# Quarters of two weight matrices on a second transfer queue, a longer run of zero products at the start, key features in half pieces, and another hand-written order

## The chip, the core and the metric

The kernel runs on one core of one Trainium2 chip. Its engines work side by side and meet only at semaphores: PE multiplies matrices, DVE and ACT do elementwise work, POOL (GpSimd) does a little of the same, SP issues transfers, and 16 DMA engines move the data. The metric is the device time of one execution in microseconds, as a median over runs.

## The reference, cut to what matters

Everything is float32 except the sketches S1, S2 and the four weight matrices, which arrive as float64 and are turned into float32 on the chip.

```python
# attention: q, k, v are (4, 4, 1088, 32); S1, S2 are (8, 32)
phi(x) = outer product of (S1 x) and (S2 x), 64 numbers for each token
kv  = sum over tokens of phi(k) v       # 64 x 32 for each head
z   = sum over tokens of phi(k)         # 64 for each head
x   = (phi(q) kv) / (phi(q) z + 1e-6)   # (4352 tokens, 128)
# feed-forward: w1, w2 are 128 x 1024, w3 is 1024 x 1024, w_out is 1024 x 128
out = (((x w1) * (x w2)) w3) w_out
```

The kernel first multiplies w3 by w_out (a 1024 x 128 matrix, here "the folded weight"), so that the feed-forward part is three products for each slice of 128 hidden columns: a, b, and the sum over slices o.

## The kernel before, in words

**The work as steps.** `make_steps` registers about 970 small steps, each with a name and a few instructions. The kernel then runs through the string `ORDER` and emits the steps in that order (lines 1173 to 1181); a scheduling dependency ties each instruction to the one before it on the same engine, so `ORDER` is the program order of PE, ACT, DVE, POOL and SP at once. There is no planner at run time: an engine that reaches an instruction whose data is not there waits, and everything behind it on that engine waits too.

**Names.** `kB.` steps make the keys' sums of batch B (0 to 3): `max`, `g`, `lead`, `rest` split the keys into a leading part and a rest (L471 to L484, DVE); `gram` multiplies keys with keys on PE (L497, L498: 36 calls each way, every float32 product being two matrix instructions and two weight loads); `Gm` to `Gb`, `T`, `N` turn that into scaling matrices in small DVE and PE steps; `kT`, `ab`, `abc` or `abt` make the sketches, `kp` the features (L515, on POOL for batch 0 and on DVE for the others), `kv` and `kvr` the sums with v on PE. `kr0` and `kr1` are the last 64 tokens of batches 0,1 and 2,3. `qG.` steps make the attention output of token group G (0 to 7, two to a batch, and `r` for the remainders); their last step `qG.xT` (ACT) writes the transposed activations that the feed-forward products of group G read. `gG.Ca`, `gG.Cb` are the products a and b of slice C (L1099, L1109), `gG.Cc` copies a out of PSUM (ACT), `gG.Cm` multiplies (DVE, L1115), `gG.Co` adds to the output (L1121). `s.` steps prepare the sketches; `s.split` runs on POOL.

**Weights.** Slice n of the weights is loaded into one of three buffers called `raw` as raw 64-bit words by `wN.load`: n = 0, 1 are halves of w1 and w2, n = 2 is w_out, n = 3 to 10 are 128 rows of w3. The last two kinds are loaded by four transfers of 32 partitions each (L303, L310), all issued by SP. ACT reads the words in `wN.c` (L325), `wN.s` (L329), `wN.m` (L333), DVE joins them in `wN.j` (L344) and `wN.a` (L349). For w3, `fN.t` transposes on DVE (L377) and `fN.m` makes the folded weight on PE (L383). A `raw` buffer can be loaded again when its `c` and `m` are done. Keys and values have one buffer each (`k`, `v`), so `k1.load` must wait until `k0.gram1` and the other readers of batch 0 are done.

**The start.** Before the first feed-forward product nothing else can feed PE for long, and `warmN` steps (L176) put bf16 products of zeros between its waits; `WARM` holds how many.

Of the kernel before, what the change touches and what calls it, by code (L numbers as in the profile page):

```python
# [25 lines left out]
WARM = [15, 5, 3, 1, 6, 15, 4, 2, 5]  # L26

BY_PE = ()

# [4 lines left out]
c.zeros v0.zero c.ident c.mask k0.zero k0.load0 k0.loadr k0.load1 s.load c.act q0.load s.zero v0.loadr w0.load  # L34
k0.max0 w1.load k0.max1 k0.nat1 kr0.load warm0 k0.tr1 k0.g0 k0.g1 k0.lead0 k0.kT1 k0.lead1 kh1.load k0.nat0
k0.rest0 s.words k0.rest1 warm1 k0.gram0 s.pair q0.tr s.split k0.gram1 q1.tr s.lead w0.c v0.load q0.max k0.tr0
k0.Gm s.T k0.Gt k0.kT0 w0.j k1.zero s.P k1.load q0.l2 s.blk k0.Ga s.blkh warm2 k0.ab1 k0.Gb q0.l1 s.Pp k1.loadr
q0.A0 k0.ab0 w2.load q0.rm k0.T0 k0.T1 k0.abc0 kr0.tr k0.abc1 k0.Ta k0.kp0 warm3 q0.C0 w1.c k1.kT1 q1.max w1.m
k0.Tb q0.sma q0.restT kr0.kT k0.Ts w0.m k0.kp1 warm4 k0.kv0 k1.max k0.N0 k0.N1 w0.s q0.sta w3.load k0.Na q0.sha
w1.s k0.Nh k0.Nb q0.sla kr1.load warm5 q0.A1 k0.Nl k0.Nf kr0.ab q0.sca k0.kv3 q0.smy kr0.abc q0.al k0.kv1 kr0.kp  # L40
q0.sty q0.C1 q0.phi w4.load q1.l2 k0.kv2 k0.kvr v1.zero q1.l1 q0.shy warm6 q0.pt0 k0.kvm q0.C1t q0.sly k0.kzt
q0.pt1 q0.pc0 q0.scy v1.load q0.p01 q1.A0 k0.kz q0.pc1 q0.p2 warm7 q0.x q1.rm q0.p12 w1.j w3.c q0.dn q0.de w2.c
q1.sm q1.C0 q0.rc q1.st q0.xs w0.a q0.xt q0.xT q1.sh w2.m k1.g w1.a warm8 g0.1a g0.1b w2.j g0.1c w5.load w2.s
k1.lead g0.0a g0.1m kr1.tr g0.6a kr1.kT g0.0c k1.rest w3.s g0.0b w2.a kr1.ab g0.6b g0.6c w3.m g0.5a g0.0m g0.6m
g0.7a g0.5c w6.load q1.sl kr1.abc k1.kT0 g0.5b w3.j g0.7b g0.5m q1.load w4.c k1.gram0 w3.a g0.7c k1.ab w4.m
q1.sca q1.scy f0.t k1.gram1 w5.c w7.load k1.gram2 q1.al q1.p01 g0.2a q1.p2 w4.s k2.zero g0.7m q1.p12 kh2.load
g0.4a w4.j g0.2c q1.dn f0.m g0.4c w4.a w6.c k2.load q1.de k1.Gm f1.t v1.loadr w5.m g0.2b g0.4b q1.rc g0.2m f0.o
w5.s w10.load f1.m k1.Gt q1.bs q2.tr w6.m q1.phi g0.0o k1.abt f1.o w6.s w8.load q1.pt1 k1.Ga q2.max q1.pt0 w5.j
g0.3a q1.pc0 g0.4m q1.pc1 k2.loadr q1.x k1.kp1 g0.1o q1.xT w5.a q2.l2 g1.1a g0.3c k1.Gb g0.3b f2.t g1.1c q2.l1
k1.T0 k1.T1 g1.5a g0.3m f2.m k1.Ta g1.5c k1.kp0 w7.c w7.m w6.j g1.1b k1.Tb g1.6a w6.a f2.o w7.s w9.load k1.kv0  # L50
g1.1m k1.kv2 k1.kv3 k1.kv1 w8.c w7.j k1.kvr g0.2o f3.t w8.s g1.5b w7.a f3.m g1.6c k1.kvm k1.Ts g1.5m w8.j g1.6b
f3.o f4.t k1.N0 w9.c k1.N1 g1.4a g1.6m g1.4b k1.Na g1.4c k2.max w9.s f4.m g1.4m w8.m k1.Nb g1.0a k2.g w9.j f4.o
g1.0b k1.Nf q2.rm g1.0c w10.c k2.lead g0.3o k1.Nl k1.Nh g1.3a g1.0m k2.rest g1.2a g1.3c w9.m g0.4o q3.tr w8.a
k2.gram0 k2.gram1 k2.kT1 q2.C0 f5.t k2.kT0 k2.gram2 q3.max q2.A0 k2.ab k3.zero k3.loadr v2.zero w9.a kr1.kp
q3.l2 v2.load f5.m g1.2c q2.At q3.l1 q2.Ct q2.sm q3.rm g1.7a f5.o w10.s q2.st f6.t g1.3b w10.m g0.5o q2.sh w10.j
f6.m q2.sl g1.3m q2.sca q2.scy q2.al q3.A0 q2.p01 f6.o q3.C0 g1.7c w10.a g1.2b q2.p2 f7.t g1.7b q2.p12 q2.dn
f7.m k2.Gm q2.de q1.restT q2.rc q2.load q2.bs q3.At v2.loadr q3.Ct g0.6o kh3.load q2.phi f7.o g0.7o k2.abt
q2.pt0 k3.load g0.oT q2.pt1 g1.2m k1.kzt g1.0o g0.st k1.kz q2.pc0 q3.sm g1.7m q2.pc1 g1.2o k2.Gt q3.st g1.5o
q3.sh q3.sl q2.x k2.kp0 g1.3o q2.xT q3.sca k3.max g2.7a g2.1a k3.g k2.Ga q3.p01 k2.kp1 g2.7b g2.1c g2.7c g1.1o
q5.tr g1.6o q5.max q3.al k3.lead g1.4o q4.tr g1.7o k2.Gb g2.5a g2.7m q4.max g2.1b q3.scy k3.rest g2.5b k2.kv0  # L60
q3.p2 k3.gram0 g2.1m q3.p12 g2.5c k3.gram1 k3.kT0 g2.5m k2.kv3 k2.kv1 k2.kv2 g1.oT k2.kvr k3.gram2 v3.zero
v3.load k2.kvm q3.dn k2.T0 k2.T1 g2.2a k3.Gm k2.Ta g2.3a k2.Tb v3.loadr g2.2c k2.Ts q3.de q4.l2 g1.st q3.rc
k2.N0 q3.bs k2.N1 q3.phi g2.2b q4.l1 g2.3c g2.0a g2.2m k2.Na g2.3b g2.0c k2.Nb q3.pt1 k2.Nh k3.kT1 g2.0b g2.3m
q3.pt0 q4.rm g2.6a k2.Nf g2.0m g2.4b g2.6c k3.Gt k2.Nl q3.pc0 g2.4a q3.pc1 q3.x q4.A0 q3.xT q4.C0 g2.4c k3.ab
g2.0o k3.abt g2.4m g3.3a g2.6b g2.2o g2.6m k3.Ga g3.3b q4.At g3.3c q4.sm g2.5o q4.st q4.Ct g3.2b g3.3m q4.sh
g3.2a k3.kp0 k2.kzt g2.1o g3.2c q5.l2 g3.2m g3.4a k3.kp1 g2.4o g3.4c k2.kz q4.sl q5.l1 g3.4b q4.sca k3.Gb g3.6a
q4.p01 g3.4m q5.A0 q4.al k3.T0 k3.T1 g3.1a k3.Ta q5.At g2.6o q4.scy g3.1c q5.sm g3.6c q5.rm g3.1b q2.restT
q3.load g2.3o g3.1m k3.Tb g3.0b q4.p2 q4.p12 g3.6b q4.dn q4.de k3.Ts q5.st g3.0a q5.sh q3.restT g2.7o g3.0c
g3.0m q5.C0 q4.rc g3.6m q5.sl k3.kv0 k3.kv1 g2.oT k3.kv3 k3.kv2 q4.bs k3.kvr g2.st q5.Ct g3.5a q5.sca q5.p01
g3.7b g3.5c q6.tr g3.0o q4.phi g3.5b k3.kvm q7.tr g3.3o q5.al qr.max g3.2o q5.scy qr.l2 g3.5m q5.p2 q4.pt0  # L70
q5.p12 g3.6o q5.dn q4.pc0 qr.l1 g3.7a q4.pt1 g3.7c g3.1o q4.pc1 g3.7m q4.x q5.de q5.rc q5.bs g3.4o q4.xT k3.N0
k3.N1 g4.3b k3.Na qr.rm g4.3a k3.Nh k3.Nf k3.Nb q5.phi g4.0a g4.3c g3.5o g4.3m g4.0c q5.pt0 g4.5a g4.5b g4.5c
q5.pc0 q5.pt1 g4.5m g3.7o q5.pc1 g4.0b g4.4a g4.0m g3.oT g4.4b g4.4c g3.st g4.2a g4.4m k3.Nl g4.7a q6.max g4.0o
qr.C0 qr.A0 q5.x qr.Ct qr.At q7.max g4.5o q5.xT qr.sm g4.2c g4.2b g4.7c q6.l2 g4.7b g4.2m q6.l1 qr.st g5.0a
g4.7m qr.sh g4.6a g5.0c qr.sl q6.rm k3.kzt g4.6b qr.sca k3.kz g4.6c qr.al qr.p01 g5.0b g4.6m q6.A0 g5.0m q6.C0
q6.At qr.scy qr.p2 q7.l2 g4.1a qr.p12 qr.dn qr.de qr.rc g4.2o g4.1c q7.l1 g4.6o q7.rm g4.3o q6.sm qr.bs g4.1b
g5.2a g4.1m qr.phi g5.2b g5.2c q6.st qr.pt0 q6.sh g5.7a qr.pc0 q6.sl q6.Ct g4.4o g5.2m qr.pt1 q6.sca g4.1o
qr.pc1 q6.al g5.7c g5.7b q7.A0 q7.C0 q7.At q6.p01 g5.7m qr.x q6.scy q6.p2 q6.p12 g5.5a q6.dn q6.de q6.rc g4.7o
g5.5c q6.bs g5.6a g4.oT g5.6b g4.st g5.6c qr.xT g5.0o g5.6m q7.sm g5.5b q7.st g5.4a g5.5m q7.sh g5.4b g5.4c
q6.phi g5.5o q7.Ct g5.1a g5.4m q6.pt0 g5.3b q6.pc0 q6.pt1 g5.3a q6.pc1 g5.1c q6.x g5.3c g5.3m g5.1b q6.xT g5.6o  # L80
g5.1m q7.sl g5.4o q7.sca g5.1o g5.3o g6.1a g5.2o g6.1c g6.1b g6.4a g6.1m q7.scy g6.6a q7.al g6.4c q7.p01 g6.4b
g6.6c g5.7o g6.4m q7.p2 g6.6b g5.oT q7.p12 g6.0a g5.st g6.6m q7.dn g6.0b g6.0c g6.5a g6.0m g6.3a g6.5c g6.3b
g6.3c g6.5b g6.3m q7.de gr.2b g6.5m g6.0o q7.rc q7.bs g6.2a q7.phi gr.2a g6.2c g6.4o gr.2c gr.2m g6.6o g6.2b
gr.0a g6.2m q7.pt1 gr.0b gr.0c q7.pt0 gr.0m g6.7a q7.pc0 g6.7b g6.7c q7.pc1 q7.x g6.7m g6.5o q7.xT g7.1a g7.1b
g7.1c g7.0a g7.1m g6.2o g7.3a g6.3o g7.3c g7.0c g7.0b g6.1o g7.0m g6.7o g7.3b g6.oT g7.4a g6.st g7.3m g7.4b
g7.4c g7.2b g7.4m g7.2a g7.6a g7.2c g7.2m g7.0o g7.6c g7.2o g7.5a g7.1o g7.5c g7.6b g7.7a g7.6m g7.5b g7.7c
gr.5a g7.5m g7.7b gr.6a g7.7m g7.5o gr.6c gr.5c g7.3o gr.6b gr.5b g7.6o gr.5m gr.6m gr.4b gr.4a g7.4o gr.4c
gr.4m gr.1b gr.1a g7.7o gr.1c gr.1m gr.3a g7.oT gr.3b gr.3c gr.7a g7.st gr.3m gr.0o gr.7c gr.6o gr.2o gr.5o
gr.7b gr.3o gr.7m gr.1o gr.4o gr.7o gr.oc gr.ot gr.oT gr.st
# [7 lines left out]
def make_steps(ctx, tc, q, k, v, S1, S2, moe_w1, moe_w2, moe_w3, moe_w_out, out):  # L97
    nc = tc.nc
    dve, act, pe, pool, sp = nc.vector, nc.scalar, nc.tensor, nc.gpsimd, nc.sync
    B, H, S, D = q.shape  # L100
# [191 lines left out]
    def conv(n):  # L292
# [3 lines left out]
        def _():  # L296
# [4 lines left out]
            elif n == 2:  # L301
                for t in range(4):
                    sp.dma_start(raw[n][t * 32:(t + 1) * 32],  # L303
                                 bass.AP(tensor=moe_w_out.tensor, offset=moe_w_out.offset + t * 256 * DM,
                                         ap=[[DM, 32], [32 * DM, NC], [1, DM]]))
            elif n - 3 in BY_PE:
                sp.dma_start(raw[n], moe_w3[(n - 3) * 128:(n - 2) * 128])
            else:
                for t in range(4):
                    sp.dma_start(raw[n][t * 32:(t + 1) * 32],  # L310
                                 bass.AP(tensor=moe_w3.tensor, offset=moe_w3.offset + (n - 3) * 128 * DF + t * 256,
                                         ap=[[DF, 32], [32 * DF, 4], [1, 256]]))
# [898 lines left out]
```

## Time and profile before

| What | us |
|---|---|
| Median of 13 runs | 281.68 (279.6 to 284.61) |
| The profiled execution | 282.83 |
| Its span, first to last instruction | 281.0 |
| PE busy in the span | 265.0 |
| DVE busy | 186.0 |
| ACT busy | 113.1 |
| POOL busy | 11.4 |
| First feed-forward product starts | 33.59 |
| Last feed-forward product ends | about 275.4 |

A row of a timeline gives the start, the length, the engine, the line, the operation with its output and inputs, the count, and in brackets the idle time before it with what ended that time. In a table of windows, PEclk is the share of full speed that the throttle granted to PE, and the DMA share is how busy the 16 DMA engines were.

### The profile page before, as it was taken

The page shows a single profiled execution, that of the slowest core. Times are in us where ns is not written, and L with a number is a line of the kernel's source. Part 1 is how long each engine was busy: PE and PEld are TensorE (multiplying, and loading weights), DVE is VectorE, ACT ScalarE, POOL GpSimd, SP SyncE. Part 2 cuts the span into 40 slices and gives each one's busy share as a digit, 9 for nine tenths or more (in the row PEclk, how much of TensorE's full clock was granted, in tenths as well). Part 3 has the DMA queues.
Part 4 walks back from the last instruction along what each step waited for, and adds up shares of the span by engine and source line. Part 5 has one row for each costly group of instructions (what it writes and reads, how often), then busy time and mean ns, then how long its engine had stood idle before and what let it go on. Part 6 is the DMA issues. An engine that isn't in the chain of part 4 may idle for free.

```text
span 281.0 us, 5298 instructions
## 1 busy us (share of the span) xinstructions
PE 265.0 (94%) x2134; PEld 149.5 (53%) x2134; DVE 186.0 (66%) x420; ACT 113.1 (40%) x180; POOL 11.4 (4%) x41
## 2 busy tenths in 40 slices
PE   7997998799997999979999999999999999999992
PEld 5885746456657663534444545444544445344571
DVE  4779989498989989956398855476773265121430
ACT  3675698667592422033231143163123222322121
POOL 2451000000001000000000000000000000000000
PEclk9999999799999999979999999999999999999999
DMA  7999999998600273050002200200020020001011
GB/s 211 314 248 217 214 198 249 218 219 168 127 1 9 75 193 79 2 119 0 2 0 80 39 1 0 37 2 1 2 37 0 0 41 0 0 15 22 0 20 38
DMA packets 32168, 22.50 MB, mean 80 GB/s; under 512 B 21392, under 2 KB 26640, under 8 KB 32144
## 3 DMA queue, kind: packets, MB, share of 16 engines
q1 hardware_dynamic: 31600, 21.64, 34.6%
q10 hardware_dynamic: 544, 0.52, 0.6%
q8 instruction: 17, 0.28, 0.5%
q14 instruction: 7, 0.06, 0.1%
HBM read 19.93 MB, written 2.23 MB: 79 GB/s over the span
## 4 chain that ended last, share of the span: by engine, by line
PE 82%; DMA 9%; SPq 3%; issue 3%; ACT 1%; DVE 0%; ACTq 0%
PE a_ps L1099 22%; PE b_ps L1109 21%; PE ps_o L1121 20%; DMA raw<-in_moe_w_dram 6%; PE ps_w3o L383 6%; PE ps_x L1065 3%; DMA raw<-in_moe_w_out_dram 3%; PE ps_c L810 3%; PE ps_ph L1020 2%; PE ps_g L492 2%; PE ps_kv L590 1%; SPq L1077 1%; PE ps_ab L565 1%; DMA out_dram<-oT 1%; SPq L300 1%
## 5 line engine op out<-in xcount | busy, mean ns | idle before, releaser
L1115 DVE TENSOR_TENSOR ab<-ffa,b_ps 128x512 f32<-128x512 f32 (+1 forms) x72 | 46.8, 652 | 62.8 <-PE b_ps L1109 48.6
L1104 ACT COPY ffa<-a_ps 128x512 f32<-128x512 f32 (+1 forms) x72 | 39.9, 564 | 98.7 <-PE a_ps L1099 93.1
L1099 PE MATMUL a_ps<-xT,w 128*128 128x512 f32 (+1 forms) x144 | 70.4, 585 | 0.4 <-ACT xT L1057 0.4
L1109 PE MATMUL b_ps<-xT,w 128*128 128x512 f32 (+1 forms) x144 | 69.7, 578 | 0.0
L1121 PE MATMUL ps_o<-ab,w3o 128*128 128x512 f32 (+1 forms) x144 | 67.4, 574 | 0.0
L1109 PEld LDWEIGHTS b_ps<-xT,w 128*128 128x128 f32 x144 | 26.8, 193 | 28.9 <-issue 25.3
L1099 PEld LDWEIGHTS a_ps<-xT,w 128*128 128x128 f32 x144 | 26.1, 192 | 26.5 <-issue 20.1
L1121 PEld LDWEIGHTS ps_o<-ab,w3o 128*128 128x128 f32 x144 | 26.1, 190 | 26.2 <-issue 23.1
L383 PEld LDWEIGHTS ps_w3o<-wo,w3T 128*128 128x128 f32 x128 | 16.2, 199 | 6.8 <-issue 5.5
L383 PE MATMUL ps_w3o<-wo,w3T 128*128 128x128 f32 x128 | 16.9, 286 | 2.5 <-issue 2.5
L325 ACT ACTIVATE cv_c<-raw 128x1024 f32<-128x1024 f32 x11 | 12.9, 1181 | 6.6 <-DMA raw<-in_moe_w_dram 5.4
L333 ACT ACTIVATE sg<-raw 128x1024 uint16<-128x1024 uint32 x11 | 15.1, 1377 | 0.0
L329 ACT CAST sg<-cv_c 128x1024 f16<-128x1024 f32 x11 | 14.9, 1372 | 0.0
L1026 ACT COPY pT<-ps_ph 128x512 f32<-128x512 f32 (+1 forms) x18 | 9.9, 567 | 7.9 <-PE ps_ph L1020 7.9
L492 PE MATMUL ps_g<-kk 128*32 128x64 f32 x288 | 10.9, 233 | 1.9 <-issue 1.9
L492 PE MATMUL ps_g<-k,kk 128*32 128x32 f32 x288 | 10.4, 200 | 1.5 <-issue 1.5
L1020 PEld LDWEIGHTS ps_ph<-ident,ph 128*128 128x128 f32 x68 | 8.3, 140 | 6.6 <-issue 4.6
L176 PE MATMUL idle_ps<-zeros 128*128 128x256 bf16 x56 | 9.9, 326 | 1.6 <-DVE zeros L151 1.1
L492 PEld LDWEIGHTS ps_g<-kk 128*32 128x32 f32 x288 | 9.0, 114 | 3.6 <-issue 2.4
L492 PEld LDWEIGHTS ps_g<-k,kk 128*32 128x32 f32 x288 | 9.7, 117 | 2.0 <-issue 2.0
L1020 PE MATMUL ps_ph<-ident,ph 128*128 128x128 f32 x68 | 10.0, 273 | 0.0
L377 DVE STREAM_TRANSPOSE w3T<-w3c 128x1024 f32<-128x1024 f32 x8 | 9.9, 1234 | 0.0
(199 smaller groups left out, 291.4 us busy)
## 6 DMA issues: line engine op xcount, KB each, us to landing
raw<-in_moe_w_dram SPq DMA_DIRECT2D x32, 256.0 KB, 7.9
qh<-in_q_dram SPq DMA_DIRECT2D x4, 544.0 KB, 4.0
raw<-in_moe_w_dram SPq DMA_DIRECT2D x4, 512.0 KB, 6.5
out_dram<-oT SPq DMA_DIRECT2D x32, 64.0 KB, 2.0
kh<-in_k_dram SPq DMA_DIRECT2D x12, 128.0 KB, 7.4
k<-in_k_dram SPq DMA_DIRECT2D x3, 512.0 KB, 7.6
v<-in_v_dram SPq DMA_DIRECT2D x12, 128.0 KB, 2.8
raw<-in_moe_w_out_dram SPq DMA_DIRECT2D x4, 256.0 KB, 7.9
```

The source lines that it names most:

```text
L176: pe.matmul(t[:, :256], zeros[:, :128], zeros, start=True, stop=True)
L325: act.mul(shape(x["c"], 1, True), words(1).bitcast(F32), 2.0 ** -112)
L329: act.copy(bview(sign_bits[n % 2].bitcast(F16)[:, 1:], [[2, 1024]]), x["c"])
L333: act.mul(shape(sign_bits[n % 2].bitcast(U16), 2, True), words(0).bitcast(U32), 2.0 ** -29)
L383: pe.matmul(t["o"], w3T[ko][:, c], wo[:, c], start=c == 0, stop=c == NC - 1)
L492: pe.matmul(o[h * D:(h + 1) * D], lhs, rhs, start=start, stop=stop, skip_group_check=True)
L1020: pe.transpose(t[:, j * 128:(j + 1) * 128], ph_cols(j, p), ident)
L1099: pe.matmul(x["a"][:, :w], w_of(0, c), xT[g][:, c0:c0 + w], start=True, stop=True)
L1104: act.copy(x["s"][:, :w], x["a"][:, :w])
L1109: pe.matmul(x["b"][:, :w], w_of(1, c), xT[g][:, c0:c0 + w], start=True, stop=True)
L1115: dve.tensor_mul(ab_sb[g, c][:, c0:c0 + w], x["s"][:, :w], x["b"][:, :w])
L1121: pe.matmul(o_ps[g][:, :n], w3o[:, c], ab_sb.pop((g, c))[:, :n], start=c == 0, stop=c == NC - 1)
```

## The change

1. `wN.load` of w_out and w3 keeps quarters 0 and 2 on SP. A new step `wN.load2` issues quarters 1 and 3 from POOL.
2. `k0.kp0` and `k0.kp1`, one POOL instruction each of 1024 columns, become `kp0a`, `kp0b`, `kp1a`, `kp1b` of 512 columns.
3. `WARM` is changed: 22 zero products at the start instead of 15, and 54 instead of 56 in all.
4. `kT` is kept per batch, so that batch 1's transposed keys can be made while batch 0's are in use.
5. `ORDER` is new throughout. At the start, the key sums' products of batch 1 (`k1.ab`, `k1.gram0` to `gram2`) stand ahead of the first feed-forward product (now `g0.7a`); before, they stood behind twelve of them. `w1` is loaded ahead of `w0`, both after batch 0's values. `k1.load` is ahead of `w0` and `w2` on SP. The folds come in the order f0, f2, f1, f4, f3, f5, f6, f7.

```diff
-WARM = [15, 5, 3, 1, 6, 15, 4, 2, 5]
+WARM = [22, 4, 5, 1, 10, 1, 6, 2, 3]
+QUEUE2 = "pool"
...
-c.zeros v0.zero c.ident c.mask k0.zero k0.load0 k0.loadr k0.load1 s.load c.act q0.load s.zero v0.loadr w0.load
-k0.max0 w1.load k0.max1 k0.nat1 kr0.load warm0 k0.tr1 k0.g0 k0.g1 k0.lead0 k0.kT1 k0.lead1 kh1.load k0.nat0
-k0.rest0 s.words k0.rest1 warm1 k0.gram0 s.pair q0.tr s.split k0.gram1 q1.tr s.lead w0.c v0.load q0.max k0.tr0
-k0.Gm s.T k0.Gt k0.kT0 w0.j k1.zero s.P k1.load q0.l2 s.blk k0.Ga s.blkh warm2 k0.ab1 k0.Gb q0.l1 s.Pp k1.loadr
-q0.A0 k0.ab0 w2.load q0.rm k0.T0 k0.T1 k0.abc0 kr0.tr k0.abc1 k0.Ta k0.kp0 warm3 q0.C0 w1.c k1.kT1 q1.max w1.m
-k0.Tb q0.sma q0.restT kr0.kT k0.Ts w0.m k0.kp1 warm4 k0.kv0 k1.max k0.N0 k0.N1 w0.s q0.sta w3.load k0.Na q0.sha
...
+c.zeros s.zero k0.zero k0.load0 k0.loadr c.ident k0.load1 c.mask s.load c.act q0.load kh1.load k0.max0 s.words
+k0.g0 k0.lead0 k0.nat1 s.pair k0.nat0 warm0 k0.tr1 k0.rest0 s.split q0.tr k0.tr0 k0.kT1 k0.max1 s.lead k0.gram0
+k0.kT0 q0.max q1.tr q0.l2 s.P s.T k0.g1 q0.restT k0.lead1 s.blk k0.rest1 warm1 k0.ab1 s.Pp k0.gram1 k0.abc1
+q0.l1 k0.kp1a k1.kT0 k0.ab0 k0.Gm v0.zero v0.load v0.loadr kr0.load w1.load k0.Gt q0.rm k0.abc0 k0.Ga s.blkh
+w1.m k0.Gb k0.kp0a warm2 q0.A0 k0.T0 k1.kT1 k0.T1 q0.C0 k0.Ta k0.kp1b q1.max k0.Tb kr0.tr q0.sma warm3 k0.N0
+kr0.kT k1.zero k1.loadr k1.load w0.load w2.load q1.load k0.Ts k0.kp0b w1.c k1.max k0.kv0 k0.kv2 k0.N1 kr0.ab
+w3.load w3.load2 k0.Na kr0.abc w1.s q0.sta kr1.load k0.Nh k1.g k0.Nf k0.Nb q0.sha warm4 q0.A1 k0.Nl k0.kv3 w1.j
+kr0.kp q0.C1 q0.smy q1.l2 k0.kv1 q0.sla q0.sty q0.sca w2.load2 warm5 k0.kvr q0.shy q1.l1 q0.C1t q0.al w0.c
+q0.sly q0.phi warm6 k1.ab w0.m q0.p01 warm7 q0.pt1 q0.scy k0.kvm q0.pt0 q0.p2 q1.rm w5.load w5.load2 k0.kzt
+k0.kz q0.p12 q0.pc0 warm8 q1.C0 k1.lead q0.pc1 w3.c q0.dn k1.rest q1.A0 w0.s q0.x q0.de q1.sm w0.j q0.rc w2.c
+k1.gram0 k1.abt q0.xs k1.gram1 q1.st w1.a q0.xt k1.gram2 q0.xT q1.sh w3.s g0.7a w0.a k2.zero k2.loadr g0.7b
...
-                for t in range(4):
-                    sp.dma_start(raw[n][t * 32:(t + 1) * 32],
-                                 bass.AP(tensor=moe_w3.tensor, offset=moe_w3.offset + (n - 3) * 128 * DF + t * 256,
-                                         ap=[[DF, 32], [32 * DF, 4], [1, 256]]))
+                quarter(sp, 0)
+                quarter(sp, 2)
...
+        if n >= 2 and n - 3 not in BY_PE:
+            @step(f"w{n}.load2")
+            def _():
+                for t in (1, 3):
+                    quarter({"pool": pool, "act": act, "sp": sp}[QUEUE2], t)
...
-                @step(f"k{b}.kp{half}")
-                def _(half=half):
-                    f["kp", half] = sb("kp", [128, 4 * H, r, r], bufs=2)
-                    x = f["abs", half]
-                    k_phi(f["kp", half], x[:, 0], x[:, 1], pool)
+                for part in "ab":
+                    @step(f"k{b}.kp{half}{part}")
+                    def _(half=half, part=part):
+                        if part == "a":
+                            f["kp", half] = sb("kp", [128, 4 * H, r, r], bufs=2)
+                        x, g = f["abs", half], slice(0, 2 * H) if part == "a" else slice(2 * H, 4 * H)
+                        k_phi(f["kp", half][:, g], x[:, 0, g], x[:, 1, g], pool)
```

## The prediction

> **What bounds the kernel now.** I read the page first, then the chain of waits in order of time, then the windows at its holes, then the timelines of the start.
>
> ```profile
> span 281.0 us, 5298 instructions
> ## 1 busy us (share of the span) xinstructions
> PE 265.0 (94%) x2134; PEld 149.5 (53%) x2134; DVE 186.0 (66%) x420; ACT 113.1 (40%) x180; POOL 11.4 (4%) x41
> ```
>
> PE sets the end. From the first feed-forward product (33.59) the chain stays on PE to 275.4 and has three holes over 1 us, all called "issue": PE waited for no data.
>
> ```profile
> 47.40 1.00 PE ps_w3o L383 x9
> 48.41 2.55 issue
> 50.95 1.86 PE ps_w3o L383 x7
> ...
> 86.88 1.51 issue
> ...
> 119.73 1.92 issue
> 122.20 3.25 PE a_ps L1099 x4
> ```
>
> The first hole lies inside one step (f0.m, 16 products, cut at nine). Counting products by the program, the holes stand near numbers 602, 988 and 1376, and a smaller one (0.52 us at 26.1) at 349: about 3, 5, 8 and 11 times 128. Each product is a matrix instruction and a weight load, so these are multiples of 256 instructions; the instruction queue moved 17 packets of 16 KB for PE's 4268. I read it so: crossing a multiple starts the fetch of the block after the next multiple, and a hole comes when PE gets there first. Crossing to resumption: 17.0 to 26.6 and 43.3 to 50.95 (9.6 and 7.7 us, DMA engines full), 84.3 to 88.39 and 117.6 to 121.9 (4.1 to 4.3, DMA idle). Each of the last three comes after a gram, 144 products within some 2.7 us. After two holes the clock is slow, too (columns: window, busy PE, PEld, DVE, ACT, POOL, PEclk, DMA share, GB/s):
>
> ```profile
> 50.90:52.60 1.70, 1.65 (x7) 1.65 (x8) 0.00 (x0) 0.05 (x1) 0.00 (x0) 0.51 1.06 217
> 52.60:56.00 3.40, 3.40 (x11) 1.62 (x11) 1.46 (x4) 2.72 (x3) 0.00 (x0) 0.74 1.07 228
> ```
>
> Here 7 fold products took 1.86 us instead of 0.78, four halves of b 2.55 instead of 1.72, the next fold 1.97 instead of 1.78: 2.1 us lost.
>
> The 33.6 us before the first product are a chain of short steps. Its timelines show a gap of 0.88 us behind the zeros, and DVE blocked while POOL makes key features: a 32x32 operation that takes 0.18 elsewhere took 1.74 and ended with POOL's first of two.
>
> ```profile
> 1.06 3.38 PE L176 MATMUL idle_ps<-zeros 128*128 128x256 bf16 x15 [1.06 <-DVE zeros L151]
> 5.33 1.09 PE L529 MATMUL ps_kt<-ident,nat 128*128 128x128 f32 x4 [0.88 <-ACT nat L523]
> ```
>
> ```profile
> 16.27 3.87 POOL L515 TENSOR_TENSOR kp<-kab 128x1024 f32<-128x1024 f32 x2 [4.02 <-ACT kab L546]
> ...
> 16.54 1.74 DVE L137 SCALAR_TENSOR_TENSOR T_p<-T_g,T_t 32x32 f32<-32x32 f32 x1
> ...
> 20.98 1.35 DVE L140 TENSOR_REDUCE k_g<-k 128x1 f32<-128x1152 f32 x1 [0.79 <-DMA k<-in_k_dram]
> ```
>
> **1. The start, -2.0 us.** Fifteen zero products took 3.38 us, so 22 reach to 6.0, when the first transposes are ready (nat1 at 4.57, now behind s.words' 0.75): no gap. Gram products run at 40 ns until 9.9 us and at 22 ns after it; all 144 at 22 ns are 3.2 us instead of 4.4. But gram1 now stands behind s.T and ab1: s.words now precedes the copies on ACT (data in by 4.4, 0.75 long), so s.pair moves from 8.1 to 5.3 on DVE and takes 0.5; s.split takes 3.4 on POOL (8.68 to 12.1 before, 5.8 to 9.2 now); s.P and s.T take 1.0 on PE, so s.T ends at 10.2; s.blk 0.3 and k0.rest1 0.7 on DVE end at 11.2; gram1 takes 1.6 and ends at 13.1 (before 11.84). Then on DVE s.Pp 1.4 and kT0 0.6 to 13.25, the G steps with q0.rm 1.5 to 14.75, kT1 0.6 to 15.4, T's first two operations to 15.8. Its shift is the operation that took 1.74 above: it now waits for half a feature instruction (0.98, half of 1.96) that started at 15.4, not for a whole one, and is done at 16.5 (before 18.28). q1.max 0.6 and Tb 0.35 end at 17.45, k1.max (1.3) when the keys land, some 18.3, so k0.Na starts at 19.6 (before 22.45). From there DVE's own sum decides: Na to the end of xs was 8.65 us; added are k1.lead 0.8, k1.rest 1.27, w0.j 0.6, k1.abt 0.62: 11.95, so xs ends at 31.6 (before 31.1). On PE q1.C0 (1.75) and x (2.2) end at 30.9, gram0 and gram1 (0.6 to 1.05 each) at 32.1 to 33.0, xt 0.45, copy 0.58: first product at 33.7 to 34.6, I take 34.3, 0.7 later. In exchange the 2.7 us that k1.gram and ab hold at 42.72 to 45.42 are gone from the packed part. Net -2.0; bounds -3.5 (gram in 0.6, no wait) and +1.5 (next point and transfers).
>
> **2. The fetch holes, -6.2 and +0.5.** In the new order number 476 (4th multiple) falls in k1.gram1, 604 in f0.m, 14 us later: over 9.6, so the hole of 2.55 and its 2.1 of slow clock go. From 860 to 988 lie f5.m 1.8, four products 3.4, two grams 1.2 to 2.1: at least 6.4, over 4.1, so 1.51 goes. From 1244 to 1372 there are 2 to 3 us (k3's three grams and T), under 4.2: that hole stays with its slow clock, 0. New risk: 348 falls at about 23.2, 476 at about 31.8; with 7.7 to 9.6 the block comes at 30.9 to 32.8, so 0 to 1.0, I take 0.5, more if the clock falls.
>
> **3. DVE as second bound, +1.5.** With PE earlier, folds are due earlier: f5.m about 77 (before 89.68), f6.m 86 (94.14), f7.m 90 (99.16). DVE needs 2.9 us a slice (0.6, 1.13, 1.16). Summing its steps from rows, DVE has 27.6 us done at 34.3, 6.7 idle, and 69 done at the end of f5.t: 75.7 if never idle again, 1.3 ahead of PE; 0.6 ahead at f6. Before, DVE idled 3.7 of the 60 us from 60 to 120. I take 1.5, bounds 0 and 4. k1.lead and k1.rest are covered by PE's own start; that cover is in the sum.
>
> **4. The second queue, 0.** Before, PE waited for no weight, so faster loading alone saves nothing. SP issued a quarter in 0.31 to 1.01 us, landing 4.9 to 10.4 later. Behind w3.load2 on POOL stand kr0.kp (for kvr) and w2.load2; it waits for w1.c (18.7, as w3.load did at 18.79). SP holds w0, w2 and q1 behind k1.load, which waits for gram1 (13.1, before 14.35). A POOL issue is in no row: nearest are SP's 0.3 to 1.0 and POOL's 1.96; two of w3's land by 18.8 + 4 + 7.8 = 30.6 at the dear end. ACT then has w3.c, w0.s, w2.c (3.7 us) ahead of xT, needed at 33.4: bounds 0 and +1. I stay at the SP row.
>
> Whether two queues are faster: loads of 128 partitions moved 341 GB/s (5 to 10 us, share 0.97), mostly quarters 212 (20 to 25, share 1.12), so quarters are slow with engines full. [...]
>
> **5. The end, -0.4.** ob waited to 276.02 for g7's store, 0.6 after the last product. Fourteen instead of twelve products of 0.43 now follow g7.7o.
>
> **Sum:** -2.0 - 4.65 - 1.5 + 0.5 + 1.5 - 0.4 = -6.55; from 282.83 that is 276.3. The execution lies 1.15 over the median (281.68); I forecast 276.0.
>
> **Rivals.** *The holes move.* For: 476 is reached within a microsecond of the fetch's limit. If the block comes at 32.8 and the clock falls (2.1), and DVE idles 2 more: 276.0 + 0.5 + 2.1 + 1.4 = 280.0. *POOL's quarters come late (slower).* Place: w3.c and w2.c stand ahead of q0.xT on ACT, then all of PE. Each microsecond of landing beyond 29.7 costs one; from about 6 us beyond, the gain is gone. Landing at twice the SP row (18.8 + 4 + 15.6 = 38.4) costs 8.7: 284.7. For: no row; against: POOL is 4% busy, its waits are short. *The zeros don't do what they are for:* gram stays at 40 ns, since the start is no sharp row; 1.2 on the chain, 277.2.
>
> **Numbers.** Forecast 0.48, holes 0.22, POOL late 0.20, zeros 0.10. About 0.5% (1.4 us) is what a measurement here can tell, that is 280.3 to 283.1. Faster: 0.48 + 0.10 + half of the holes, 0.69 less 0.02 for tails, 0.67; same 0.12; slower 0.21. Low end: no DVE loss, no hole at 476 and a start of -3.5 give 272.5; high end reaches half into POOL late: 284. The forecast's own range is 273 to 279.
>
> **What would show it.** Right: first product near 34.3 with k1.gram before it; no "issue" in f0.m nor in k2's gram, one near k3's; k0.Na near 19.6. Wrong: ACT idle ahead of w3.c or w2.c for a DMA; PE waiting for w3T or DVE in f5 to f7; POOL rows of over 2 us.

## The result: slower, not faster

The changed kernel takes 285.56 us (median of 11 runs, 283.78 to 287.24); the kernel before, run beside it, 282.06 (median of 48). The ratio is 1.016 (95% interval 1.013 to 1.019). This ratio and those below compare the fast executions of a kernel with those of the kernel before that ran beside it, so they differ a little from the quotient of the medians. The forecast was 276.0 with a range of 272 to 284: wrong in sign, and the time lies outside the range.

The profiled execution of the changed kernel took 282.48 us, 1.3 us less than the quickest of those eleven, so it is a lucky one. Its mean granted clock was 0.987; that of the eleven was 0.968 to 0.982. The head of its page:

```profile
span 280.7 us, 5321 instructions
## 1 busy us (share of the span) xinstructions
PE 264.6 (94%) x2132; PEld 148.2 (53%) x2132; DVE 185.7 (66%) x420; ACT 112.3 (40%) x180; POOL 23.5 (8%) x61
```

PE is as busy as before; POOL's added 12 us are mostly the quarters it issues. The chain of waits (start, length, what) shows the loss:

```profile
18.88 1.08 ACT cv_c L335
...
19.98 0.31 SPq L316
...
20.33 17.36 DMA raw<-in_moe_w_dram
...
38.90 1.32 ACT sg L339
...
40.24 1.14 ACT cv_c L335
41.38 0.48 ACT xT L1069
...
41.90 2.07 PE a_ps L1111 x2
43.98 1.71 PE b_ps L1121 x2
45.69 1.71 PE a_ps L1111 x2
47.39 1.20 PE b_ps L1121 x2
48.59 0.86 PE a_ps L1111 x2
```

The last quarter of w3 lands 17.4 us after its issue. It is one of the pair that SyncE (SP) issues. In the transfers' views from 20 us to 21 and from 21 to 22, the last column is the median time to landing of w3's two quarters on SyncE and of its two on GpSimd (POOL):

```profile
raw<-in_moe_w_dram SPq DMA_DIRECT2D x2, 256.0 KB, 16.0
...
raw<-in_moe_w_dram POOLq DMA_DIRECT2D x2, 256.0 KB, 11.5
```

GpSimd's pair took 4.5 us less by this measure. ACT reaches w3.c near 29.3, waits 8.55 us, then does w0.s and w2.c, and only then q0.xT, on which all feed-forward products wait. ACT's row at w3.c and PE's at its first product, before and after:

```profile
30.84 2.22 ACT L325 ACTIVATE cv_c<-raw 128x1024 f32<-128x1024 f32 x2 [2.24 <-DMA raw<-in_moe_w_dram]
...
33.59 1.12 PE L1099 MATMUL a_ps<-xT,w 128*128 128x512 f32 x2 [0.36 <-ACT xT L1057]
```

```profile
37.88 1.12 ACT L335 ACTIVATE cv_c<-raw 128x1024 f32<-128x1024 f32 x1 [8.55 <-DMA raw<-in_moe_w_dram]
...
41.90 2.07 PE L1111 MATMUL a_ps<-xT,w 128*128 128x512 f32 x2 [5.52 <-ACT xT L1069]
```

ACT waited for w3 in the kernel before, too, by 2.24 us. In the changed kernel the first product starts at 41.90 (before 33.59, forecast 34.3), 5.5 us after PE has run dry, and the next four pairs take 2.07, 1.71, 1.71 and 1.20 instead of 0.86 each. The windows give the reason (PEclk is the third column from the end):

```profile
42.00:44.00 2.00, 2.00 (x3) 0.97 (x4) 0.41 (x1) 1.09 (x1) 0.00 (x0) 0.50 0.00 0
46.00:49.00 3.00, 3.00 (x6) 1.19 (x5) 1.78 (x5) 1.57 (x2) 1.46 (x2) 0.67 0.66 138
```

The clock fell to 0.50 in the wait: 5.5 + 3.25 = 8.75 us. Against that stand the fetch holes. PE's timeline at the places of before's holes, and the new one:

```profile
1.07 4.88 PE L178 MATMUL idle_ps<-zeros 128*128 128x256 bf16 x22 [1.07 <-DVE zeros L153]
6.33 1.38 PE L539 MATMUL ps_kt<-ident,nat 128*128 128x128 f32 x8 [0.38 <-ACT nat L533]
...
34.40 0.28 PE L502 MATMUL ps_g<-kk 128*32 128x64 f32 x4 [1.44 <-issue]
...
57.35 1.95 PE L393 MATMUL ps_w3o<-wo,w3T 128*128 128x128 f32 x16
```

f0.m is whole (16 products in one row), there is no hole at k2's or k3's gram, and one of 1.44 us in k1.gram1, which costs nothing here since ACT ends later. From the first product to the end of the span it is 238.8 us instead of 247.4. Of these 8.6 us the rows give 8.5: k1's gram and ab done earlier 2.7, three holes 6.0, their low clock 2.1 and 1.5, the last copy's wait 0.6, less 3.25 of low clock after the new wait and 1.1 of waits for DVE near 80. So in the profiled execution nearly everything that the change gained behind the first product was lost ahead of it.

### The profile page after: what moved, and what is told of

Same layout as the page of the kernel before. It is cut to its first block, busy times and chain, and to the rows that moved or that the text cites. A ratio compares the mean times of both kernels' runs of the same rounds, so it can differ in the third digit from the quotient of the medians.

```text
span 280.7 us, 5321 instructions
## 1 busy us (share of the span) xinstructions
PE 264.6 (94%) x2132; PEld 148.2 (53%) x2132; DVE 185.7 (66%) x420; ACT 112.3 (40%) x180; POOL 23.5 (8%) x61
## 4 chain that ended last, share of the span: by engine, by line
PE 81%; DMA 11%; ACT 2%; DVE 2%; SPq 1%; issue 1%; ACTq 0%; DVEq 0%
PE ps_o L1133 21%; PE a_ps L1111 21%; PE b_ps L1121 20%; DMA raw<-in_moe_w_dram 6%; PE ps_w3o L393 4%; DMA kh<-in_k_dram 3%; PE ps_c L822 3%; PE ps_x L1077 3%; PE ps_ph L1032 2%; DMA qh<-in_q_dram 2%; PE ps_g L502 2%; ACT cv_c L335 1%; PE ps_ab L550 1%; PE ps_kv L602 1%; PE ps_ab L577 1%
## 5 line engine op out<-in xcount | busy, mean ns | idle before, releaser
L1111 PE MATMUL a_ps<-xT,w 128*128 128x512 f32 (+1 forms) x144 | 71.3, 586 | 5.5 <-ACT xT L1069 5.5
L1121 PE MATMUL b_ps<-xT,w 128*128 128x512 f32 (+1 forms) x144 | 71.5, 584 | 0.0
L1111 PEld LDWEIGHTS a_ps<-xT,w 128*128 128x128 f32 x144 | 26.7, 194 | 36.5 <-issue 24.2
L1133 PEld LDWEIGHTS ps_o<-ab,w3o 128*128 128x128 f32 x144 | 26.4, 190 | 27.1 <-issue 23.8
L393 PEld LDWEIGHTS ps_w3o<-wo,w3T 128*128 128x128 f32 x128 | 15.2, 192 | 2.6 <-issue 1.7
L393 PE MATMUL ps_w3o<-wo,w3T 128*128 128x128 f32 x128 | 15.6, 276 | 0.0
L316 POOL DMA_DIRECT2D raw<-in_moe_w_dram x16 | 9.7, 609 | 38.7 <-ACT sg L343 18.0
L502 PE MATMUL ps_g<-kk 128*32 128x64 f32 x288 | 9.8, 225 | 1.4 <-issue 1.4
L359 DVE CUSTOM_DVE_ANT_0 w3c<-w3c,sg 128x2048 uint16<-128x2048 uint16 x8 | 9.7, 1218 | 0.6 <-ACT sg L343 0.6
L502 PEld LDWEIGHTS ps_g<-kk 128*32 128x32 f32 x288 | 8.3, 109 | 2.9 <-issue 1.9
```

The lines of the kernel that those rows point to most:

```text
L393: pe.matmul(t["o"], w3T[ko][:, c], wo[:, c], start=c == 0, stop=c == NC - 1)
L502: pe.matmul(o[h * D:(h + 1) * D], lhs, rhs, start=start, stop=stop, skip_group_check=True)
L1111: pe.matmul(x["a"][:, :w], w_of(0, c), xT[g][:, c0:c0 + w], start=True, stop=True)
L1121: pe.matmul(x["b"][:, :w], w_of(1, c), xT[g][:, c0:c0 + w], start=True, stop=True)
L1133: pe.matmul(o_ps[g][:, :n], w3o[:, c], ab_sb.pop((g, c))[:, :n], start=c == 0, stop=c == NC - 1)
```

## The experiments

Four theories were told apart. **Q** (called A in the first four): GpSimd's queue delivers late. **B**: the order of the steps costs the time. **V** (first called C): the transfer engines are full, and what counts is how many bytes stand ahead of w3, whichever queue carries them. **S**: between k0's two grams PE has little to do, the clock falls, and k1.load with all loads behind it starts later. SyncE's own pair landing last in the change's profile already speaks against Q.

**e1_sp: the second pair of quarters on SyncE's queue.**

```
-QUEUE2 = "pool"
+QUEUE2 = "sp"
```

> The changed kernel with one edit: the second pair of quarters goes to SyncE's queue, as the first pair does; order, zeros and halves stay. Theory A (the GpSimd queue lands late: 17.4 us for w3, ACT's w3.c waits 8.55, PE 5.5, and then runs 3.25 at a low clock): w3.c no longer waits over 1 us, first feed-forward product at 36.3, span 281 - 8.7 = 272, the median 274 to 277, ratio to before 0.97 to 0.985. Rival B (the new order itself costs it, with w3.c, w0.s and w2.c ahead of q0.xT): ACT still waits and the ratio stays 1.01 to 1.02. Rival C (all quarters come too late when the transfer engines are full, whichever engine issues them): w3.c waits 4 us or more, ratio 1.00 to 1.01.

Measured: 281.52 us, ratio to before 1.003 (1.000 to 1.006). That is 1.3% under the change's ratio, but not the 0.97 to 0.985 of theory Q: in the profile the first product comes at 40.76. One thing is unclean: w2's second pair now stood in SyncE's line behind w3 and kr1 and was issued at 29.26. f1 mends this.

**e2_act: the second pair on ScalarE's queue.**

```
-QUEUE2 = "pool"
+QUEUE2 = "act"
```

> The changed kernel with the second pair of quarters issued by ScalarE. If any second queue would do it (rival C), the wait at w3.c stays at 5 us or more and the ratio near 1.01. If it is GpSimd's kind of queue alone (A), quarters land 5 to 10 us after issue, first product near 36.5, and the time is that of e1 plus ACT's own issue time, 2 x 0.4 to 0.9 per slice, of which only w3's, w2's and w5's stand ahead of q0.xT: 275 to 279.

Measured: 287.06 us, 1.019 (1.012 to 1.025). ScalarE is itself in the chain: in the profiled execution (289.84, the longest of its four) it did nothing from 30.1 to 37.9 but issue w5's pair (2.31 us, begun at 35.59), with q0's copies in line behind; first product at 46.85. ScalarE's queue is no better here, but for a reason of its own, so this run says little on Q.

**e3_later: w3.c and w2.c behind the first products.**

```
-q0.pc1 w3.c q0.dn ... q0.rc w2.c k1.gram0 ... g0.2c q1.scy w4.load
+q0.pc1 q0.dn ... q0.rc k1.gram0 ... g0.2c w3.c w3.s w3.j ... w2.c w2.m w2.j w2.s w2.a w4.load
```

> The changed kernel with GpSimd's queue, but w3.c, w2.c and what hangs on them stand behind the first feed-forward products in the order instead of ahead of q0.xT. Theory A: quarters land as late as before (12 to 18 us), but only f0 needs them, so the first product comes at 35 to 36.3, PE keeps its clock, ACT has some 6 us more to do beside the products and waits for w3 to 37.9: 276 to 279. Rival C (the full transfer engines also hold back what PE needs) : the first product stays near 41. Rival B (order): no statement on the wait, PE loses as much elsewhere, 282 or more.

Measured: 283.27 us, 1.006 (1.002 to 1.010), against a forecast of 276 to 279. In the profiled execution ACT no longer waited for w3 ahead of q0.xT, and yet the first product came at 42.49. It is the longest of the ten (286.52), so its chain does not stand for the median. From ab1 and gram1 on:

```profile
12.47 1.97 PE ps_ab L550 x8
14.44 3.05 PE ps_g L502 x72
17.49 1.90 PE ps_ab L550 x8
```

gram1 took 3.05 us instead of the 1.72 of the change's profile, and the steps to 32.7 about twice their time: the clock stood at 0.50 from 12.4 to 32.9. This is where theory S came from. The slow clock is not all: the three executions with a mean clock of 0.994 took 281.5 to 281.9, still no less than the kernel before (280.94). The moved conversions cost PE elsewhere, as B had it: in the profile it waits 3.41 us for ACT's copies ahead of a product at 53.68.

**e4_before_pool: the kernel before with quarters 1 and 3 on GpSimd's queue.**

```
-                    sp.dma_start(raw[n][t * 32:(t + 1) * 32],
+                    (sp, pool)[t % 2].dma_start(raw[n][t * 32:(t + 1) * 32],
```

> The kernel before with one edit: quarters 1 and 3 of each slice go to GpSimd's queue; order, zeros and whole halves stay. There too w3.c and w2.c stand ahead of q0.xT on ACT. Theory A: w3's quarters, issued near 18.8, land at 34 to 36.5, so the first product moves from 33.6 to 37 to 39.5 and the clock may fall behind it: ratio 1.012 to 1.03. Rival B (the new order is at fault): ratio 0.995 to 1.005.

Measured: 285.26 us, 1.015 (1.010 to 1.021), as theory A said, but not by its way: in the profile ACT started w3.c at 34.20 without a wait for data, and the first product came at 39.08 because the clock stood at 0.50 from 15.1 to 28.8. So the time fits A and the profile fits S; the run does not tell them apart.

**f1_fifo: all four quarters on SyncE's queue, behind one another.**

```
-QUEUE2 = "pool"
+QUEUE2 = "sp"
-w0.load w2.load q1.load ... q0.sca w2.load2 warm5
+w0.load w2.load w2.load2 q1.load ... q0.sca warm5
```

> The changed kernel with all four quarters of a slice on SyncE's queue right behind one another (w2's second pair too, which stood behind w3's in e1). Theory Q (GpSimd's queue alone makes w3 and w2 late): w3 lands 7 us after its issue, near 28, first feed-forward product at 36 to 37, ratio to before 0.97 to 0.99. Theory V (the transfer engines are full: from k1.load on, 0.5 + 1.05 + 1.05 + 0.54 + 1.05 MB for k1, w0, w2, q1 and w3 stand in the new order ahead of w3's end, 4.2 MB at 0.22 MB a microsecond, whichever engine issues them): w3 lands some 18.7 us after k1.load's start (14.7 to 16.5), at 33.5 to 35.5, first product at 37.5 to 39.5, ratio 0.99 to 1.005.

Measured: 282.89 us, 1.005 (1.001 to 1.009), just at the dear end of theory V's forecast (w3 in by 33.5 to 35.5, first product at 37.5 to 39.5) or past it: w3.c at 35.74, first product at 39.77. With no GpSimd queue at all, ACT still waits over 7 us for w3:

```profile
35.74 1.12 ACT L335 ACTIVATE cv_c<-raw 128x1024 f32<-128x1024 f32 x1 [7.18 <-DMA raw<-in_moe_w_dram]
```

Theory Q falls here. The DMA view of the stretch from k1.load's issue to the start of w3.c, in f1 (14.4 to 36 us) and in the changed kernel (14.7 to 38):

```profile
DMA packets 3693, 4.85 MB, mean 225 GB/s; under 512 B 1029, under 2 KB 2565, under 8 KB 3690
```

```profile
DMA packets 3144, 5.11 MB, mean 219 GB/s; under 512 B 986, under 2 KB 2010, under 8 KB 3141
```

The rate is the same by one queue or two. w3 is late because 4 to 5 MB move ahead of it or beside it, at 0.22 MB a microsecond.

**f2_q1_later: one load moved, GpSimd's queue kept.**

```
-w0.load w2.load q1.load k0.Ts ... w5.load w5.load2 k0.kzt
+w0.load w2.load k0.Ts ... w5.load w5.load2 q1.load k0.kzt
```

> The changed kernel with GpSimd's queue as it is; one edit: q1.load (544 KB) is issued behind w5's quarters instead of ahead of w3's. Theory Q: w3.c still ends its wait near 37.9, first product near 41.9, ratio 1.01 to 1.02. Theory V: 0.54 MB less ahead is 2.4 us at 0.22 MB a microsecond, so w3.c starts near 35.5 and the first product comes near 39.5; ratio 1.00 to 1.01.

Measured: 280.54 us, 0.996 (0.991 to 1.001): one load of 0.54 MB moved is worth 2.0% against the change, more than theory V's 2.4 us. The stretch now holds 4.04 MB (16.7 to 35 us), and the wait is 3.81:

```profile
34.78 1.18 ACT L335 ACTIVATE cv_c<-raw 128x1024 f32<-128x1024 f32 x1 [3.81 <-DMA raw<-in_moe_w_dram]
```

The first product comes at 38.89, 3.0 earlier than in the change's profile, after 2.33 us without work. The clock did not fall in this wait, so the pairs take 0.86 and the 3.25 us of low clock are gone too. Between the two profiled executions only 2.3 us of this are left at the end: PE now waits 3.0 us for DVE near 77 (1.1 in the change), and the clock is at 0.50 for some 3.4 us behind that. How the 5.6 us (2.0%) between the two ratios are made up is open.

**f3_start: k0's two grams together.**

```
-s.split q0.tr k0.tr0 k0.kT1 k0.max1 s.lead k0.gram0 ... s.P s.T k0.g1 q0.restT k0.lead1 s.blk k0.rest1 warm1 k0.ab1 s.Pp k0.gram1
+s.split k0.max1 k0.g1 k0.lead1 k0.rest1 q0.tr k0.tr0 k0.kT1 s.lead k0.gram0 k0.gram1 ... s.P s.T q0.restT s.blk warm1 k0.ab1 s.Pp
```

> The changed kernel with GpSimd's queue as it is; one edit: k0's two grams stand together on TensorE, ahead of s.P, s.T and ab1, and what gram1 needs on VectorE stands ahead of q0.tr. Theory S (in the new order the products between the two grams leave gaps in most executions, the clock falls to 0.50 and gram1 takes 3.0 instead of 1.7 us, which holds back k1.load, w0, w2, q1 and w3 behind it): gram1 ends near 11 at full clock, k1.load is issued near 11 instead of 14.7 to 16.5, the transfer engines do not fall idle at 14 to 17, w3.c starts 2 to 4 us earlier, ratio 1.00 to 1.005. Theory Q: the start does not matter as long as w3 lands 17 us after its issue behind w1.c, ratio 1.01 to 1.02.

Measured: 280.47 us, 0.998 (0.994 to 1.002). Both grams take 3.47 us together and end at 11.5; k1.load is issued at 11.67; ACT waits for no weight ahead of q0.xT, with GpSimd's queue as it is. The clock fell all the same, later (18.4 to 28.6). k1.load is 3.0 us ahead of the change's profile, in which the clock was full at that point; so the run shows what an earlier start of the loads is worth, and leaves open what the fall of the clock costs.

**f4_all: f1, f2 and f3 together.** No new lines.

> The three edits f1, f2 and f3 together: all quarters on SyncE's queue, q1.load behind w5's quarters, k0's grams together. Theories V and S: k1.load at 11, w3 landed at 11 + 3.7 MB / 0.22 = 28, ACT waits for no weight ahead of q0.xT, first product at 34 to 36, ratio 0.97 to 0.985. If something else in the new order costs the time (for example VectorE's work in front of q0.xs), the ratio stays at 0.99 or more.

Measured: 278.24 us, 0.989 (0.981 to 0.996), above the 0.97 to 0.985 of theories V and S. No wait for weights is left, but the first product comes at 38.41, not at 34 to 36. The windows show what holds it now:

```profile
13.00:14.00 1.00, 1.00 (x11) 1.00 (x11) 0.93 (x4) 0.32 (x2) 0.00 (x0) 1.00 1.04 387
14.00:15.00 1.00, 1.00 (x8) 0.87 (x8) 0.96 (x4) 0.98 (x3) 0.87 (x1) 0.64 1.04 283
20.00:21.00 1.00, 1.00 (x6) 1.00 (x6) 0.00 (x0) 0.00 (x0) 0.00 (x0) 0.50 1.11 186
28.00:29.00 1.00, 1.00 (x32) 0.67 (x25) 0.83 (x4) 0.97 (x2) 0.00 (x0) 1.00 1.11 202
```

The clock is 0.50 from 14.3 to 27.9, and PE, busy nearly all that time, has become the chain of the start.

**f5_clock: f4 with more zero products and T earlier.**

```
-WARM = [22, 4, 5, 1, 10, 1, 6, 2, 3]
+WARM = [22, 8, 8, 1, 10, 1, 6, 2, 3]
-k0.ab1 s.Pp k0.abc1 q0.l1 ... k0.Gm ... k0.Gt q0.rm k0.abc0 k0.Ga s.blkh w1.m k0.Gb ... warm2 q0.A0 k0.T0 k1.kT1 k0.T1
+k0.ab1 q0.l1 k0.abc1 k0.Gm k0.Gt k0.Ga s.blkh k0.Gb ... s.Pp ... q0.rm k0.abc0 ... k0.T0 k0.T1 warm2 k1.kT0 q0.A0 k1.kT1
```

> f4 with two more edits in the stretch from 11 to 17 us: warm1 has 8 zero products instead of 4 and warm2 8 instead of 5, and k0's G steps stand ahead of s.Pp and q0.rm on VectorE, so that T comes before A0. Theory S (in windows of some 3.4 us in which the products are small and far apart the clock is set to 0.50, for f4 from 14.2 to 27.9): the clock stays at 1.00 from 6 to 40 us, xT comes some 3 to 4 us earlier, first feed-forward product at 34 to 36 instead of 38.4, ratio to before 0.97 to 0.98. If the clock falls all the same, 0.985 to 0.99 as f4; if the added zeros only delay the chain, 0.99 to 0.995.

Measured: 276.02 us, 0.979 (0.974 to 0.985), the best of all. The two edits were not tried one by one. In the profile the clock is full to 20.3 and low to 27.1 (so it did fall, for 6.8 us instead of 13.7), and the first product comes at 36.61:

```profile
14.00:17.00 3.00, 2.94 (x31) 2.67 (x31) 2.86 (x8) 1.89 (x3) 1.82 (x3) 1.00 0.98 328
21.00:27.00 6.00, 6.00 (x77) 4.59 (x78) 4.82 (x22) 3.12 (x5) 0.68 (x1) 0.50 1.12 229
```

The low clock became shorter with the two edits together. That small products far apart set it, as theory S has it for this run, was not shown.

**f6_clock_pool: f5 on two queues.**

```
-QUEUE2 = "sp"
+QUEUE2 = "pool"
```

> f5 with the second pair of quarters on GpSimd's queue again. Theory Q (that queue lands late and costs PE's start): ACT waits 4 us or more for w3, ratio 1.5% or more above that of f5. Theory V (bytes ahead in the engines decide, not the queue): w3's wait under 2 us, ratio within 0.7% of f5's.

Measured: 277.13 us, 0.984 (0.978 to 0.989): 0.4% above f5, with intervals that overlap. Theory V's ratio held; its wait of under 2 us for w3 did not (2.67). With enough bytes moved away from w3 GpSimd's queue costs little, and it brings nothing. What is left of its price is seen on ACT and PE:

```profile
32.59 1.22 ACT L335 ACTIVATE cv_c<-raw 128x1024 f32<-128x1024 f32 x1 [2.67 <-DMA raw<-in_moe_w_dram]
```

```profile
36.78 1.13 PE L1111 MATMUL a_ps<-xT,w 128*128 128x512 f32 x2 [1.50 <-ACT xT L1069]
```

**e8_before_q1: the kernel before with q1.load ahead of w3.**

```
-q0.sta w3.load k0.Na ... g0.5m q1.load w4.c
+q0.sta q1.load w3.load k0.Na ... g0.5m w4.c
```

> The kernel before with one edit: q1.load (544 KB) is issued ahead of w3's quarters instead of behind w6's. Theory V: w3 and w2's conversions wait 2.4 us longer (0.54 MB at 0.22 MB a microsecond; w3.c began at 30.84 after a wait of 2.24), first product at 35.5 to 36.5 instead of 33.59, ratio 1.006 to 1.012, less what is not fetched later at 42. Theory Q, or one by which only the start's chain counts: 0.998 to 1.003.

Measured: 282.22 us, 1.001 (0.997 to 1.005), under theory V's 1.006 to 1.012. The wait is there (w3.c at 35.43 after 3.12, first product at 38.16, though this execution also had the clock at 0.50 from 15.7 to 29.3), but the fetch holes shrink as PE comes later: 0.73 us in f0.m instead of 2.55, without low clock behind it. The load is also gone from its old place at 42. The cost was given back; how much by each is open.

**e5_before_zeros: the kernel before with 22 zero products.**

```
-WARM = [15, 5, 3, 1, 6, 15, 4, 2, 5]
+WARM = [22, 5, 3, 1, 6, 15, 4, 2, 5]
```

> The kernel before with one edit: 22 instead of 15 zero products at first. As forecast: the gap of 0.88 ahead of the first transposes goes, at most 0.9 us saved, ratio 0.997 to 1.0. Fetch theory (blocks of 256 PE instructions, counted along the program): all PE instructions move by 14, so each issue hole comes seven products earlier in the program: that of f0.m after its second fold product instead of its ninth, about 0.8 us earlier and as long as before or longer. If holes belong to the step and not to the count, it stays after the ninth.

Measured: 283.75 us, 1.004 (1.000 to 1.008): no gain, if anything a loss. The hole of f0.m moved as the fetch theory said, seven products earlier, and is a little longer (2.87 instead of 2.55, by the chain of waits):

```profile
49.00 0.38 PE L383 MATMUL ps_w3o<-wo,w3T 128*128 128x128 f32 x2
52.26 2.13 PE L383 MATMUL ps_w3o<-wo,w3T 128*128 128x128 f32 x14 [2.87 <-issue]
```

## Why the prediction was wrong

**Part 4, "the second queue, 0", is the step that failed.** No run shows its term of 0, with bounds of 0 and +1: the change's profile has 5.5 us of waiting and 3.25 of low clock in its place. Part 4 took SP's landing time (4.9 to 10.4 us) for a load that stands behind 4 MB; SP's two quarters of w3 took 14.7 and 17.4. Its premise, "PE waited for no weight", was true of PE and not of ACT, which waited 2.24 us for w3 two steps ahead of xT: the loads had no slack to lose. The forecast had both numbers in hand: "SP holds w0, w2 and q1 behind k1.load, which waits for gram1", and mostly quarters at 212 GB/s. Summed, 0.5 + 1.05 + 1.05 + 0.54 + 1.05 MB at 0.22 MB a microsecond from 14.7 is 33.7 for w3 on one queue, not "30.6 at the dear end"; one queue measured 35.7 (f1), and two 37.7. Of the 7.6 us by which the first product came after the forecast's 34.3, 5.5 are this wait; the other 2.1 belong to parts 1 and 2. Landing times of single loads were read from an order in which w3 stood in another place.

The rival "POOL's quarters come late" named the right place (w3.c and w2.c ahead of q0.xT), the right price (41.9 against its 43) and the right total (284.7 against 285.56), at a chance of 0.20. Its cause was not right: GpSimd's own quarters landed after 11.1 and 11.9 us, at 31.4 and 32.9, and the last one, at 37.7, was SyncE's. That its figures came so close is luck in part. Taking the queue away alone (f1) brings 1.1%, moving q1.load alone (f2) 2.0%, the grams alone (f3) 1.8%. So the order of the loads counts most, and the second queue makes it worse. A reason that fits, though no run separates it: GpSimd issued its pair of w5 (0.5 MB, 2.4 us at 0.22 MB a microsecond) at 27.9, beside SyncE's w3, while in f1 the same pair stood behind w3, and w3.c came 2.1 us earlier.

**Part 1, the start,** was right in the profiled execution: zeros to 6.0, gram at 24 ns a product (forecast 22), gram1 12.85 to 14.57, T's shift 0.18 instead of 1.74, and k0.Na at 21.0 (forecast 19.6, before 22.45; k1's keys were in 1.4 later than assumed). But it took the clock of one execution for granted. Of the six profiles with this start (the change, e1, e2, e3, f1, f2) four show the clock at 0.50 from 12.4 to 13.4 on, and gram1 at 2.9 to 3.05 us. That this makes up the 3 us between the profiled execution and the median is likely, since all eleven others have a lower mean clock, but none of them was profiled. "Zeros 22" on their own saved nothing (e5).

**Part 2, the fetch holes,** was right in kind: 2.55, 1.51 and the low clock went, and the count by instructions was shown in e5. For the fetch itself speak three packets of some 16 KB on the instruction queue (q8, the profile of the kernel before): they start at 48.25 to 48.50, 85.25 to 85.50 and 118.75 to 119.00, behind the crossings that the forecast counts at 43.3, 84.3 and 117.6, and PE resumes 2.5 to 3.1 us later (50.95, 88.39, 121.65). Two sizes were off. The third hole, which was to stay, went too: the forecast put the need at product 1372, in k3.gram2, 1.8 us behind the crossing; if the count is off by some 16, the need falls at 1390, behind three long pairs and 4.3 us after the crossing. That is an argument; no run fixes the count so closely. The hole is missing in every profile of the new order and there in every one of the old (1.23 to 1.92 us), so it goes with the order; why is open. And the new hole in k1.gram1 was 1.44 instead of 0.5, hidden here by the wait of 5.5.

**Parts 3 and 5** were of the right size: PE waited 1.1 us for DVE near 80 (forecast 1.5), and 0.7 instead of 1.3 for the last copy. For part 3 that is partly luck: PE came 7.6 us later than the forecast had it, and in f1 to f6, where the first product came at 36.6 to 39.8, PE waited 1.9 to 3.2 us for DVE between 70 and 80.

## What to carry to other kernels

Before moving loads, sum the bytes of every transfer that stands ahead of the first one that an in-order engine waits for, from the moment at which the line can start, and divide by the rate that the profile shows for such shapes; a second queue did not raise the rate here (219 GB/s with it, 225 without), and its transfers ran beside earlier loads of the first queue. Then look what that engine has in line behind the wait. And where a start consists of short products, look at the clock there: in f5, with more zeros and T earlier, it was low for 6.8 us instead of f4's 13.7, while seven more zeros alone (e5) saved nothing. Judge such a start by several executions, since one profile may show the lucky clock.

## What the runs showed of the hardware

**The low clock came in lengths near multiples of 3.42 us.** Summed over its windows, the first spell at 0.50 in the start, falls during a wait for weights left out, lasted 3.43, 3.42 and 3.43 (e1, e2, f2), 3.44 (f6), 3.40 (e5), 6.86 (f5), 10.3 (f3), 13.5, 13.5 and 13.7 (e4, e8, f4) and 20.5 us (e3): one, two, three, four and six times 3.42. What sets this length, and why executions of the same start differ, was not shown. In these spells the clock fell without a long gap of PE: the longest ahead of one of these falls was 2.5 us (e5), and in f4 it fell at 14.3 after 7.9 us without a single gap, in a stretch of small products (8 rows, 64 columns).

**Two queues moved no more than one.** 219 GB/s with GpSimd's queue beside SyncE's (the change), 225 with SyncE's alone (f1), with the engines' share at 0.96 and 0.97. Nor was f6, on two queues, faster than f5, on one (277.13 and 276.02 us). In the changed kernel a quarter's issue on GpSimd took 0.55 to 0.92 us (w3 and later slices), w2's 0.62 and 1.06.

**Issues came late in f1 and e2.** In f1 SyncE's four issues of w3 took 5.53 us (19.74 to 25.27), where two took 1.25 in the change. The second had ended at 21.78, the third began at 23.42 and ended at 23.73, the last began at 24.95: 1.64 and 1.22 us between them, while the engines' share was 0.96 to 1.14. What held SyncE there was not shown. In e2 ScalarE's first copy behind its issue of w5 came after 7.83 us without work, which the profile puts down to a landing of w_out's quarters.
